# A fused attention, norm and gated feed-forward kernel: the second group's scores moved behind the first group, kept low bits on ScalarE, normalising on GpSimd

## The chip, the cores and the metric

The kernel runs on one core of a Trainium2 chip. The time is the device time of one execution in microseconds (us). Three runs of the kernel before took 690.78, 692.34 and 692.8 us; the median is 692.34. Engines: TensorE (PE) multiplies, VectorE (DVE) and ScalarE (ACT) work on whole tiles, GpSimd (POOL) does some of the same work, SyncE (SP) issues transfers. Each takes its own instructions in the order of the program and waits on semaphores for the others.

## The reference

Causal attention for batch 4, 12 heads, 448 positions, head size 64, float32, then a root-mean-square norm and a gated feed-forward layer over 1792 tokens of width 768 (inner width 1536). The weights arrive as float64.

```python
scores = scale * np.matmul(q, k.transpose(0, 1, 3, 2))
scores = np.where(mask, -1000000000.0, scores)
attn = np.exp(scores - np.max(scores, axis=-1, keepdims=True))
attn = attn / (np.sum(attn, axis=-1, keepdims=True) + 1e-09)
x = np.matmul(attn, v)          # then (batch, position, head * 64 + d)
rms = np.sqrt(np.mean(x * x, axis=-1, keepdims=True) + 1e-06)
xn = x / rms * rms_g
g = xn @ w_gate
silu = g * (1.0 / (1.0 + np.exp(-g)))
out = (silu * (xn @ w_val)) @ w_out
```

## The kernel before

**Data.** Activations lie feature-major: a tile has 128 features on its partitions and 512 tokens side by side. A float32 product is made of rounded parts: each operand is split into a high and a low part, and three matmuls (L438 to L440: high by high, low of x, low of w) make one multiplication of 128 x 128 by 512.

**Weights.** There are 36 tiles of 128 x 768, numbered s; tile s is loaded as float64 (two 32-bit words to a value) and turned into float32 by `convert_ops` (L367): c0 scales the high word (ScalarE, L377), c1 multiplies the high word by 0, which leaves its sign (GpSimd, L378), c2 joins to it three low bits, shifted out of the low word (VectorE, L380), c3 shifts the scaled value and joins those bits to it (VectorE, L382), and the result is also stored to DRAM. `split_w` (L387) then makes the high part w_h (ScalarE, L392) and the low part w_l (VectorE at L394 for even tiles, GpSimd by `pool_op` at L102 for odd ones).

**Attention.** The work is cut into 60 units, each for two heads and one stretch of queries, in three groups that end at units 12, 24 and 60; a group's tokens go through the norm and the feed-forward layer together. The first two groups have 256 queries a unit. One unit passes through `steps_s` (scores L191, mask and negative maximum L200, exponential and its sum L203, reciprocal of the sum L212, normalising L206 on ScalarE for units 15 to 23 and L208 on GpSimd for the others), `steps_t` (transposes L248, copies out of their banks L252 or L254) and `steps_a` (products L274, copy to x L289). x is squared and summed (`square`, `rms`: matmuls with ones L336, square root L338, then four reciprocals of 128 x 128 on VectorE, L341), and split into high and low parts (L327, L328).

**Order.** The order is written out by hand. `round_steps(p)` gives the steps of one round: scores of unit p+3, products of p, the two transposes of p+1. A main loop performs one step at a time and puts weight loads, conversions, splits and multiplications between the steps; `post(d, f)` puts an instruction d ticks later. During the first group the multiplications of tiles 0 to 2 that are ready go between the steps. The rounds run on until four steps past the first group's end; then the feed-forward stage begins: three slots to a weight tile, each with two of six multiplications, and the remaining attention steps of the second group are spread over the first 108 slots (L54). Gate tiles (even) give `gr` (L452), tanh (L453) and L454; value tiles (odd) give the gated product (L462), its high part hh (L463) and low part hl (L465). The sections behind the second group (the third group, the output products, lines L567 to L735) are not touched.

Of the kernel before, what the change touches and what calls it, by code (L numbers as in the profile page):

```python
# [61 lines left out]
def attention_ffn(ctx: ExitStack, tc: tile.TileContext, qk0, qk1, qk2, v, v2, w, g, out, out2):  # L62
# [108 lines left out]
    def steps_s(p):  # L171
# [22 lines left out]
        def softmax(e, i, pss):  # L194
# [10 lines left out]
            if ENDS[0] + 3 <= p < ENDS[1]:  # L205
                pr["norms"].append(lambda: nc.scalar.mul(sp, sp, rs))  # L206
            else:
                pr["norms"].append(lambda: nc.gpsimd.tensor_scalar(  # L208
                    sp, sp, rs, 1.0, op0=ALU.mult, op1=ALU.mult))
# [157 lines left out]
    def convert_ops(s):  # L367
        if s >= NU:
# [5 lines left out]
        hf_ = raw_w.bitcast(F32)[:, :, 1]  # L374

# [11 lines left out]
    def split_w(s):  # L387
        if s < 2 * NU:
            t = wt[s]
            h = ws_p.tile([P, DM], F32R, tag="wh", name="w_h")  # L390
            l = ws_p.tile([P, DM], F32R, tag="wl", name="w_l")
            nc.scalar.copy(h, t)  # L392
            if s % 2 == 0 and s < NU or s > NU + 2 * NF and s % 2:
                post(T["wl0" if s == 0 else "wl2" if s == 2 else "wl"], lambda: nc.vector.tensor_tensor(l, t, f32(h), op=ALU.subtract))  # L394
            else:
                post(T["wl0" if s == 1 else "wl"], lambda: pool_op(l, t, ALU.subtract, f32(h)))
            wt[s] = tuple(a.rearrange("p (k m) -> p k m", m=P) for a in (h, l))
            u = s - NU
# [339 lines left out]
    def round_steps(p):  # L738

        noop = [lambda: None]  # L740
        (s_, ts) = (f or noop for f in (steps_s(p + DP), steps_t(p + 1)))
# [16 lines left out]
        ts = (ts + noop)[:2]  # L758
        return [both] + ts if p > ENDS[0] else [scores, products, ts[0]] + 2 * noop + ts[1:]
# [31 lines left out]
    with tc.manual_schedule():  # L791
# [215 lines left out]
```

## Time and profile before

| what | before |
|---|---|
| median of three runs (lowest, highest) | 692.34 us (690.78, 692.8) |
| the profiled execution's own time | 691.18 us |
| its span, mean granted TensorE clock | 689.1 us, 0.993 |
| TensorE busy | 668.7 us (97%) |
| VectorE busy | 539.4 us (78%) |
| ScalarE busy | 371.4 us (54%) |
| GpSimd busy | 359.6 us (52%) |
| TensorE waits for GpSimd's low part of w (L440) | 5.0 us in 2 waits, longest 4.5 |
| TensorE waits for ScalarE's copy of transposes (L274) | 2.8 us in 2, longest 2.6 |
| TensorE waits for VectorE's copy of transposes (L274) | 2.7 us in 4, longest 1.4 |

The profile is of one execution; a row gives the start, the duration, the engine and the line of one or several instructions, and in brackets how long the engine stood idle before it and which engine's result ended that wait. The clock that the throttle granted TensorE is a share of full speed. Adding up busy time says little here, since the engines wait for each other; a wait of TensorE is what an edit can take away or bring.

### The profile page before, as it was taken

The numbers are of one execution on the slowest core, as the hardware profiler recorded it, in microseconds if no ns is written. First come the engines' busy times: TensorE is split into PE (matmuls) and PEld (weight loads), VectorE is DVE, ScalarE is ACT, GpSimd is POOL, SyncE is SP. The second block draws the span as 40 slices with busy tenths as digits, with TensorE's granted clock in tenths as the row PEclk, the third lists the DMA queues.
The fourth block names the chain that finished last, engine by engine and source line by source line (L and its number), as shares of the span: only waits on it lengthen the run. The fifth ranks groups of instructions, "written<-read, shape, count | busy, mean of one in ns | idle before, by whom it ended". The sixth has DMA issues, their size and how long they took to land. (4 is left out here: it accounts for less than half of the span.)

```text
span 689.1 us, 11935 instructions
## 1 busy us (share of the span) xinstructions
PE 668.7 (97%) x4108; PEld 550.9 (80%) x4108; DVE 539.4 (78%) x1030; ACT 371.4 (54%) x832; POOL 359.6 (52%) x311
## 2 busy tenths in 40 slices
PE   8879899999999999999999999999999999999997
PEld 6546577777777777687877777888999999999997
DVE  4967999999997667777686968389386868679993
ACT  6958877877694535355364544434434342455550
POOL 4979446555547544747576566663363536312220
PEclk9989999999999999999999999999999999999999
DMA  7655587878777746575758565324667566562641
GB/s 250 226 176 176 163 273 259 290 253 274 241 251 275 246 144 219 189 251 181 260 170 263 185 206 179 115 101 150 187 214 250 173 251 221 176 168 74 175 138 65
DMA packets 71355, 138.80 MB, mean 201 GB/s; under 512 B 7744, under 2 KB 39232, under 8 KB 71296
## 3 DMA queue, kind: packets, MB, share of 16 engines
q1 hardware_dynamic: 71296, 138.05, 60.8%
q8 instruction: 32, 0.52, 0.3%
q14 instruction: 27, 0.22, 0.1%
HBM read 104.21 MB, written 33.82 MB: 200 GB/s over the span
## 5 line engine op out<-in xcount | busy, mean ns | idle before, releaser
L208 POOL TENSOR_SCALAR sp<-sp,rs 128x384 f32<-128x384 f32 (+3 forms) x132 | 87.6, 681 | 101.2 <-DVE rs L212 93.2
L438 PE MATMUL m_ps<-xh,w_h 128*128 128x512 f32 x282 | 120.5, 427 | 1.7 <-DVE rs L212 1.7
L440 PE MATMUL m_ps<-xh,w_l 128*128 128x512 f32 x282 | 112.0, 397 | 4.5 <-POOL w_l L102 4.5
L203 ACT ACTIVATE sp<-sp,nm 128x384 f32<-128x384 f32 (+3 forms) x168 | 87.2, 524 | 47.2 <-DVE nm L200 47.2
L439 PE MATMUL m_ps<-xl,w_h 128*128 128x512 f32 x282 | 111.4, 395 | 0.0
L102 POOL TENSOR_TENSOR a_l<-w_q,a_h 128x768 fp32r<-128x768 f32 x24 | 47.6, 1985 | 66.5 <-ACT a_h L476 66.3
L378 POOL TENSOR_SCALAR w<-w 128x768 f32<-128x768 f32 x36 | 45.4, 1262 | 47.3 <-ACT w_c L377 47.3
L274 PEld LDWEIGHTS a_ps<-pt,v_r 128*64 128x64 f32 (+1 forms) x864 | 40.9, 138 | 33.5 <-issue 13.2
L440 PEld LDWEIGHTS m_ps<-xh,w_l 128*128 128x128 f32 x282 | 53.5, 190 | 17.0 <-POOL w_l L102 5.0
L438 PEld LDWEIGHTS m_ps<-xh,w_h 128*128 128x128 f32 x282 | 53.6, 190 | 14.2 <-issue 6.1
L274 PE MATMUL a_ps<-pt,v_r 128*64 128x128 f32 (+2 forms) x864 | 57.0, 269 | 7.4 <-ACT pt L254 2.8
L252 DVE COPY pt<-t_ps 128x384 f32<-128x384 f32 (+1 forms) x71 | 42.5, 598 | 26.6 <-PE t_ps L248 26.5
L102 POOL TENSOR_TENSOR w_l<-w_r,w_h 128x768 fp32r<-128x768 f32 x30 | 59.6, 1994 | 5.6 <-ACT w_h L392 5.3
L439 PEld LDWEIGHTS m_ps<-xl,w_h 128*128 128x128 f32 x282 | 53.8, 191 | 7.9
L200 DVE CUSTOM_DVE_ANT_0 sp<-s_ps,mask 128x128 f32<-128x128 f32 (+3 forms) x136 | 49.8, 416 | 13.1 <-PE s_ps L191 12.1
L438 PE MATMUL m_ps<-hh,w_h 128*128 128x512 f32 x144 | 58.2, 404 | 0.0
L440 PE MATMUL m_ps<-hh,w_l 128*128 128x512 f32 x144 | 56.5, 392 | 0.4 <-POOL w_l L102 0.4
L439 PE MATMUL m_ps<-hl,w_h 128*128 128x512 f32 x144 | 56.2, 390 | 0.0
L248 PE MATMUL t_ps<-ident,sp 128*128 128x128 f32 (+1 forms) x309 | 50.3, 276 | 0.1
L248 PEld LDWEIGHTS t_ps<-ident,sp 128*128 128x128 f32 (+1 forms) x309 | 38.0, 139 | 14.6 <-issue 2.3
L382 DVE SCALAR_TENSOR_TENSOR w_c<-w_c,w 128x768 int32<-128x768 int32 x36 | 48.3, 1342 | 0.8
L380 DVE SCALAR_TENSOR_TENSOR w<-w 128x768 int32<-128x768 int32 x36 | 44.9, 1246 | 4.9 <-POOL w L378 4.9
(178 smaller groups left out, 1694.1 us busy)
## 6 DMA issues: line engine op xcount, KB each, us to landing
w<-in_w SPq DMA_DIRECT2D x36, 768.0 KB, 5.3
w<-w_c SPq DMA_DIRECT2D x36, 384.0 KB, 2.7
w_r<-w SPq DMA_DIRECT2D x36, 384.0 KB, 4.8
qk_r<-in_qk SPq DMA_DIRECT2D x48, 256.0 KB, 4.2
qk_r<-in_qk SPq DMA_DIRECT2D x12, 512.0 KB, 5.8
v_r<-in_v SPq DMA_DIRECT2D x12, 448.0 KB, 5.4
v_r<-in_v SPq DMA_DIRECT2D x24, 192.0 KB, 3.3
wy<-w_r SPq DMA_DIRECT2D x24, 192.0 KB, 4.7
```

Of the source, the lines that this page charges most:

```text
L102: nc.gpsimd.tensor_tensor(out_, a, b, op=op)
L200: nc.vector.tensor_tensor_reduce(out=sp, in0=ps, in1=mk, scale=nsc, scalar=3.0e38, op0=ALU.add, op1=ALU.min, accum_out=nm)
L203: post(T["exp" if p >= ENDS[0] else "exp0"], lambda: nc.scalar.activation(sp, sp, AF.Exp, bias=nm, scale=-1.0, accum_out=sm))
L208: pr["norms"].append(lambda: nc.gpsimd.tensor_scalar(sp, sp, rs, 1.0, op0=ALU.mult, op1=ALU.mult))
L248: nc.tensor.transpose(ps[:kb, at: at + P], pr["sp"][e][:, o + kb * j: o + kb * (j + 1)], ident)
L274: nc.tensor.matmul(av_ps[e * D: (e + 1) * D, p % 2, q0: q0 + n], raw_v[p][:kb, h, j, e, :], pr["pt", e][:kb, a0: a0 + n], start=(j == 0), ...
L378: (T["c1"], lambda: nc.gpsimd.tensor_scalar(hf_, hf_, 0.0, 1.0, op0=ALU.mult, op1=ALU.mult)),
L380: (T["c2" if s >= 5 else "c20"], lambda: nc.vector.scalar_tensor_tensor(out=lo, in0=lo, scalar=29, in1=hi, op0=ALU.logical_shift_right, op ...
L382: (T["c3" if s >= 5 else "c30"], lambda: nc.vector.scalar_tensor_tensor(out=ti, in0=ti, scalar=3, in1=lo, op0=ALU.logical_shift_left, op1= ...
L438: nc.tensor.matmul(ps, wh[:, k, :], mh, start=(first and k == ks[0]), stop=False)
L439: nc.tensor.matmul(ps, wh[:, k, :], ml, start=False, stop=False)
L440: nc.tensor.matmul(ps, wl[:, k, :], mh, start=False, stop=(last and k == 5))
```

## The change

Four edits. (1) The scores of units 12, 13 and 14 leave the rounds 9 to 11, and unit 12's transposes leave round 11; they are issued by a new `refill` behind unit 11's products. Rounds from unit 12 on have three steps. The attention steps that are spread over the 108 slots are 42 instead of 36. (2) For the odd tiles from 5 to 35 (16 of 36) c2 is made on ScalarE: an activation reads the top byte of the low word and writes a 16-bit integer into the high word. For the others c2 stays on VectorE and writes the high word instead of the low one. (3) Units 15 to 23 are normalised on GpSimd like the others (36 instructions). (4) w_l of tile 1 is made on VectorE instead of GpSimd.

```diff
--- before.py
+++ after.py
@@ -11,6 +11,8 @@
 F32 = mybir.dt.float32
 F32R = mybir.dt.float32r
 I32 = mybir.dt.int32
+I16 = mybir.dt.int16
+U8 = mybir.dt.uint8
 BF16 = mybir.dt.bfloat16
 ALU = mybir.AluOpType
 AF = mybir.ActivationFunctionType
@@ -202,11 +204,8 @@
                 op0=ALU.add, op1=ALU.min, accum_out=nm)
             post(T["exp" if p >= ENDS[0] else "exp0"], lambda: nc.scalar.activation(
                 sp, sp, AF.Exp, bias=nm, scale=-1.0, accum_out=sm))
-            if ENDS[0] + 3 <= p < ENDS[1]:
-                pr["norms"].append(lambda: nc.scalar.mul(sp, sp, rs))
-            else:
-                pr["norms"].append(lambda: nc.gpsimd.tensor_scalar(
-                    sp, sp, rs, 1.0, op0=ALU.mult, op1=ALU.mult))
+            pr["norms"].append(lambda: nc.gpsimd.tensor_scalar(
+                sp, sp, rs, 1.0, op0=ALU.mult, op1=ALU.mult))
 
         def norm():
             nc.vector.reciprocal(pr["rs"][:, :nb], pr["sm"][:, :nb])
@@ -372,15 +371,22 @@
         wt[s] = t
         ti, lo, hi = t.bitcast(I32), raw_w[:, :, 0], raw_w[:, :, 1]
         hf_ = raw_w.bitcast(F32)[:, :, 1]
+        flat = raw_w.rearrange("p c t -> p (c t)")
+        low = flat.bitcast(I16).rearrange("p (c t) -> p c t", t=4)[:, :, 2]
+        top = flat.bitcast(U8).rearrange("p (c t) -> p c t", t=8)[:, :, 3]
+        if s >= 5 and s % 2:
+            kept = (T["c2"], lambda: nc.scalar.activation(low, top, AF.Copy, bias=-31.0 / 64, scale=1.0 / 32))
+        else:
+            kept = (T["c2" if s >= 5 else "c20"], lambda: nc.vector.scalar_tensor_tensor(
+                out=hi, in0=lo, scalar=29, in1=hi, op0=ALU.logical_shift_right, op1=ALU.bitwise_or))
 
         return [
             (T["c0"], lambda: nc.scalar.mul(t, hf_, 2.0 ** -112)),
             (T["c1"], lambda: nc.gpsimd.tensor_scalar(
                 hf_, hf_, 0.0, 1.0, op0=ALU.mult, op1=ALU.mult)),
-            (T["c2" if s >= 5 else "c20"], lambda: nc.vector.scalar_tensor_tensor(
-                out=lo, in0=lo, scalar=29, in1=hi, op0=ALU.logical_shift_right, op1=ALU.bitwise_or)),
+            kept,
             (T["c3" if s >= 5 else "c30"], lambda: nc.vector.scalar_tensor_tensor(
-                out=ti, in0=ti, scalar=3, in1=lo, op0=ALU.logical_shift_left, op1=ALU.bitwise_or)),
+                out=ti, in0=ti, scalar=3, in1=hi, op0=ALU.logical_shift_left, op1=ALU.bitwise_or)),
             (T["c5" if s >= 5 else "c50"], lambda: nc.sync.dma_start(out=w32[s], in_=t)),
         ]
 
@@ -390,10 +396,10 @@
             h = ws_p.tile([P, DM], F32R, tag="wh", name="w_h")
             l = ws_p.tile([P, DM], F32R, tag="wl", name="w_l")
             nc.scalar.copy(h, t)
-            if s % 2 == 0 and s < NU or s > NU + 2 * NF and s % 2:
-                post(T["wl0" if s == 0 else "wl2" if s == 2 else "wl"], lambda: nc.vector.tensor_tensor(l, t, f32(h), op=ALU.subtract))
+            if s == 1 or s % 2 == 0 and s < NU or s > NU + 2 * NF and s % 2:
+                post(T["wl2" if s == 2 else "wl0" if s < 2 else "wl"], lambda: nc.vector.tensor_tensor(l, t, f32(h), op=ALU.subtract))
             else:
-                post(T["wl0" if s == 1 else "wl"], lambda: pool_op(l, t, ALU.subtract, f32(h)))
+                post(T["wl"], lambda: pool_op(l, t, ALU.subtract, f32(h)))
             wt[s] = tuple(a.rearrange("p (k m) -> p k m", m=P) for a in (h, l))
             u = s - NU
             if 0 <= u < 2 * NF:
@@ -738,7 +744,8 @@
     def round_steps(p):
 
         noop = [lambda: None]
-        (s_, ts) = (f or noop for f in (steps_s(p + DP), steps_t(p + 1)))
+        first = p < ENDS[0]
+        s_, ts = (f(n) if not first or n < ENDS[0] else [] for f, n in ((steps_s, p + DP), (steps_t, p + 1)))
         as_ = steps_a(p)
 
         def products():
@@ -749,14 +756,22 @@
         def scores():
             if p + 2 > 0:
                 post(T["lv"], lambda: load_v(p + 2))
-            s_[0]()
+            for f in s_:
+                f()
 
         def both():
             scores()
             products()
 
-        ts = (ts + noop)[:2]
-        return [both] + ts if p > ENDS[0] else [scores, products, ts[0]] + 2 * noop + ts[1:]
+        ts = (ts + 2 * noop)[:2]
+        return [scores, products, ts[0]] + 2 * noop + ts[1:] if first else [both] + ts
+
+    def refill():
+
+        steps = []
+        for p in range(ENDS[0], ENDS[0] + DP):
+            steps += steps_s(p) + ([lambda: None] * 2 if p < ENDS[0] + DP - 1 else steps_t(ENDS[0]))
+        return steps
 
     def round_of_two(p):
 
@@ -802,6 +817,8 @@
             steps += round_steps(p)
             if p + 1 in ENDS:
                 ends.append(len(steps))
+            if p + 1 == ENDS[0]:
+                steps += refill()
         steps.append(lambda: steps_t(ENDS[1] + 1)[0]())
         for p in range(ENDS[1], len(UNITS), 2):
             steps += round_of_two(p)
```

In the changed kernel the same instructions have other line numbers: scores L193, mask L202, exponential L205, normalising L207, transposes L247, copies L251 and L253, products L273, norm reciprocals L340, c2 on ScalarE L378 and on VectorE L380, c0 L384, c1 L385, c3 L388, w_h L398, w_l L400 and L104, multiplications L444 to L446, gr L458, tanh L459, hh L469.

GpSimd in the rounds of the first group, before (sp_535 and sp_536 are unit 7's two score tiles, sp_596 is unit 8's; w_l_577 is tile 1's low part, xr_556 a tile of x):

```order
L208 TENSOR_SCALAR sp_535<-sp_535,rs_534 128x128
L208 TENSOR_SCALAR sp_535<-sp_535,rs_534 128x256
L208 TENSOR_SCALAR sp_536<-sp_536,rs_534 128x128
L208 TENSOR_SCALAR sp_536<-sp_536,rs_534 128x256
L102 TENSOR_TENSOR sq_633<-xr_556 128x512
L102 TENSOR_TENSOR acc_407<-acc_407,sq_633 128x512
L102 TENSOR_TENSOR w_l_577<-w_c_455,w_h_576 128x768
L208 TENSOR_SCALAR sp_596<-sp_596,rs_595 128x128
```

and after:

```order
L207 TENSOR_SCALAR sp_535<-sp_535,rs_534 128x128
L207 TENSOR_SCALAR sp_535<-sp_535,rs_534 128x256
L207 TENSOR_SCALAR sp_536<-sp_536,rs_534 128x128
L207 TENSOR_SCALAR sp_536<-sp_536,rs_534 128x256
L104 TENSOR_TENSOR sq_633<-xr_556 128x512
L104 TENSOR_TENSOR acc_407<-acc_407,sq_633 128x512
L207 TENSOR_SCALAR sp_596<-sp_596,rs_595 128x128
L207 TENSOR_SCALAR sp_596<-sp_596,rs_595 128x256
```

w_l_577 is gone from GpSimd's queue, and the next unit's normalising follows the sum at once.

VectorE around the four reciprocals of the first group's norm, before (w64_727 is the raw tile 5, gr_1075 the first gate product):

```order
L212 RECIPROCAL rs_950<-sm_949 128x4
L341 RECIPROCAL rms_1014<-rms_1014 128x128 x4
L452 TENSOR_TENSOR gr_1075<-m_ps_579,rms_1014 128x512
L212 RECIPROCAL rs_1018<-sm_1017 128x4
L454 SCALAR_TENSOR_TENSOR t_sb_1076<-t_sb_1076,gr_1075 128x512
L380 SCALAR_TENSOR_TENSOR w64_727<-w64_727 128x768
L382 SCALAR_TENSOR_TENSOR w_c_1063<-w_c_1063,w64_727 128x768
```

and after (sp_931 and sp_932 are unit 12's score tiles, sp_961 and sp_962 unit 13's):

```order
L202 ISA sp_932,nm_928<-s_ps_934,mask_104 128x256
L202 ISA nm_928 128x1
L340 RECIPROCAL rms_926<-rms_926 128x128 x4
L202 ISA sp_961,nm_958<-s_ps_963,mask_104 128x128
L202 ISA nm_958 128x1
L202 ISA sp_961,nm_958<-s_ps_963,mask_104 128x256
L202 ISA nm_958 128x1
L202 ISA sp_962,nm_958<-s_ps_964,mask_104 128x128
L202 ISA nm_958 128x1
L202 ISA sp_962,nm_958<-s_ps_964,mask_104 128x256
L202 ISA nm_958 128x1
L458 TENSOR_TENSOR gr_990<-m_ps_579,rms_926 128x512
```

Before, the masks of four units of the second group stand ahead of the reciprocals; after, those of unit 12 alone, and unit 13's stand behind them.

GpSimd at the same place, before (the names sp_951 and sp_952 belong to unit 14, w_l_1066 is tile 3's low part):

```order
L208 TENSOR_SCALAR sp_951<-sp_951,rs_950 128x128
L208 TENSOR_SCALAR sp_951<-sp_951,rs_950 128x256
L208 TENSOR_SCALAR sp_952<-sp_952,rs_950 128x128
L208 TENSOR_SCALAR sp_952<-sp_952,rs_950 128x256
L378 TENSOR_SCALAR w64_727<-w64_727 128x768
L102 TENSOR_TENSOR w_l_1066<-w_c_748,w_h_1065 128x768
L378 TENSOR_SCALAR w64_867<-w64_867 128x768
```

and after (sp_931 and sp_932 belong to unit 12, sp_961 to unit 13, w_l_981 is tile 3's low part):

```order
L385 TENSOR_SCALAR w64_608<-w64_608 128x768
L385 TENSOR_SCALAR w64_727<-w64_727 128x768
L104 TENSOR_TENSOR w_l_981<-w_c_748,w_h_980 128x768
L207 TENSOR_SCALAR sp_931<-sp_931,rs_930 128x128
L207 TENSOR_SCALAR sp_931<-sp_931,rs_930 128x256
L207 TENSOR_SCALAR sp_932<-sp_932,rs_930 128x128
L207 TENSOR_SCALAR sp_932<-sp_932,rs_930 128x256
L385 TENSOR_SCALAR w64_845<-w64_845 128x768
L207 TENSOR_SCALAR sp_961<-sp_961,rs_960 128x128
```

Unit 12's normalising now stands behind tile 3's low part.

ScalarE behind the square root, before (sp_1019 and sp_1020 are unit 15's tiles, pt_1085 a copy for unit 13's products):

```order
L377 ACTIVATE w_c_1063<-w64_727 128x768
L392 CAST w_h_1065<-w_c_748 128x768
L453 ACTIVATE t_sb_1076<-gr_1075 128x512
L206 ACTIVATE sp_1019<-sp_1019,rs_1018 128x128
L206 ACTIVATE sp_1019<-sp_1019,rs_1018 128x256
L206 ACTIVATE sp_1020<-sp_1020,rs_1018 128x128
L206 ACTIVATE sp_1020<-sp_1020,rs_1018 128x256
L254 COPY pt_1085<-x_ps_1086 128x384
L377 ACTIVATE w_c_1091<-w64_867 128x768
```

and after (sp_1020 and sp_1021 are unit 14's, w64_727 the raw tile 5, w_h_980 tile 3's high part):

```order
L384 ACTIVATE w_c_978<-w64_727 128x768
L398 CAST w_h_980<-w_c_748 128x768
L459 ACTIVATE t_sb_991<-gr_990 128x512
L384 ACTIVATE w_c_1000<-w64_845 128x768
L398 CAST w_h_1002<-w_c_857 128x768
L378 ACTIVATE w64_727<-w64_727 128x768
L469 CAST hh_1014<-t_sb_991 128x512
L205 ACTIVATE sp_1020,sm_1018<-sp_1020,nm_1017 128x128
L205 ACTIVATE sp_1020,sm_1018<-sp_1020,nm_1017 128x256
```

L378 is the kept low bits of tile 5, now on ScalarE, between tile 4's high part and the cast hh; L206, the normalising, is gone.

## Rows read from the trace of the kernel before

**Rows 1.** Busy times by stage: stretch, length, each engine busy (instructions), TensorE clock, DMA.

```profile
41.00:48.00 7.00, 6.15 (x27) 3.97 (x27) 2.84 (x12) 0.00 (x0) 2.65 (x6) 0.51 0.59 189
78.50:82.00 3.50, 3.50 (x9) 2.73 (x10) 3.47 (x7) 0.91 (x2) 0.86 (x1) 0.51 0.28 110
...
92.00:180.00 88.00, 88.00 (x452) 68.59 (x451) 87.67 (x132) 66.39 (x152) 49.29 (x30) 1.00 0.78 266
```

**Rows 2.** Timeline near 40 us: start, duration, engine, line, operation, [idle before, releaser].

```profile
38.23 1.91 DVE L382 SCALAR_TENSOR_TENSOR w_c<-w_c,w 128x768 int32<-128x768 int32 x1
...
39.28 2.52 POOL L102 TENSOR_TENSOR w_l<-w_c,w_h 128x768 fp32r<-128x768 f32 x1
...
41.85 0.80 PE L440 MATMUL m_ps<-xh,w_l 128*128 128x512 f32 x1 [4.54 <-POOL w_l L102]
...
44.60 0.56 DVE L252 COPY pt<-x_ps 128x384 f32<-128x384 f32 x1 [4.47 <-PE x_ps L248]
...
46.08 1.55 PE L274 MATMUL a_ps<-pt,v_r 128*64 128x256 f32 x8
```

**Rows 3.** Timeline from 66 to 78 us, all engines, behind the sum of squares.

```profile
66.89 1.02 PE L336 MATMUL t_ps<-acc,ones 128*128 128x512 f32 x2
...
69.77 0.29 DVE L200 CUSTOM_DVE_ANT_0 sp<-s_ps,mask 128x128 f32<-128x128 f32 x1 [1.51 <-PE s_ps L191]
...
70.81 0.40 ACT L203 ACTIVATE sp<-sp,nm 128x128 f32<-128x128 f32 x1
...
70.97 3.35 DVE L341 RECIPROCAL rms<-rms 128x128 f32<-128x128 f32 x4
...
71.25 1.62 POOL L208 TENSOR_SCALAR sp<-sp,rs 128x128 f32<-128x128 f32 x4 [3.53 <-DVE rs L212]
...
72.70 0.30 ACT L226 ACTIVATE sm<-sm,tiny 128x4 f32<-128x4 f32 x1
...
73.46 0.93 PE L191 MATMUL s_ps<-qk_r 64*128 64x128 f32 x8
...
75.38 1.80 POOL L102 TENSOR_TENSOR w_l<-w_c,w_h 128x768 fp32r<-128x768 f32 x1
75.69 1.48 ACT L206 ACTIVATE sp<-sp,rs 128x128 f32<-128x128 f32 x4
...
77.58 0.86 PE L274 MATMUL a_ps<-pt,v_r 128*64 128x256 f32 x6 [2.62 <-ACT pt L254]
```

**Rows 4.** Timeline of TensorE alone, 86 to 92 us.

```profile
86.57 0.49 PE L248 MATMUL x_ps<-ident,sp 128*128 128x128 f32 x3
...
91.20 0.47 PE L438 MATMUL m_ps<-xh,w_h 128*128 128x512 f32 x1 [1.38 <-DVE rs L212]
```

**Rows 5.** Groups by line, 0 to 240 us: count, busy us, mean ns, idle before.

```profile
L382 DVE SCALAR_TENSOR_TENSOR w_c<-w_c,w 128x768 int32<-128x768 int32 x36 | 48.3, 1342 | 0.8
...
L380 DVE SCALAR_TENSOR_TENSOR w<-w 128x768 int32<-128x768 int32 x36 | 44.9, 1246 | 4.9 <-POOL w L378 4.9
...
L377 ACT ACTIVATE w_c<-w 128x768 f32<-128x768 f32 x36 | 33.1, 919 | 10.2 <-DMA w<-in_w 8.0 <-issue 2.2
L392 ACT CAST w_h<-w_c 128x768 fp32r<-128x768 f32 x36 | 29.6, 823 | 0.7 <-DVE w_c L382 0.7
...
L453 ACT ACTIVATE t_sb<-gr 128x512 f32<-128x512 f32 x12 | 7.6, 631 | 6.1 <-DVE gr L452 5.8
L452 DVE TENSOR_TENSOR gr<-m_ps,rms 128x512 f32<-128x512 f32 x11 | 7.5, 680 | 0.1
```

**Rows 6.** Timeline near 116 us: VectorE and GpSimd.

```profile
115.75 2.13 POOL L102 TENSOR_TENSOR w_l<-w_c,w_h 128x768 fp32r<-128x768 f32 x1 [0.74 <-ACT w_h L392]
...
116.09 2.62 DVE L380 SCALAR_TENSOR_TENSOR w<-w 128x768 int32<-128x768 int32 x1
...
120.86 0.92 DVE L380 SCALAR_TENSOR_TENSOR w<-w 128x768 int32<-128x768 int32 x1
```

**Rows 7.** Groups by line, 92 to 180 us: TensorE, last of the three multiplications.

```profile
L440 PE MATMUL m_ps<-xh,w_l 128*128 128x512 f32 x107 | 41.9, 391 | 0.0
```

## The prediction

> **What bounds the kernel now.** I read the busy times by stage first, then the timelines of the three places that the change touches, then the groups by line. From 92 to 180 us TensorE is busy all of the 88.00 us, and VectorE 87.67 of them; ScalarE has 66.39, GpSimd 49.29 [rows 1]. So no edit gains in that stretch: a lighter VectorE gives TensorE nothing that it waits for there, and an edit can only cost. What can be gained lies before 92 us. There TensorE waits 4.54 us for the low part of weight tile 1, which GpSimd makes last of a row of jobs [rows 2], then 2.62 us ahead of unit 13's products and 1.38 us ahead of a bank of the gate products [rows 3, 4]. Behind the first two waits the granted clock is 0.51 (the lower of the two levels, 1.2 GHz): from 41 to 48 us and from 78.5 to 82 us [rows 1].
>
> All sums are on the profiled execution (691.18 us: a span of 689.1 and 2.1 around it). The median of the timed runs, 692.34, is 1.2 above it, the lowest run 0.4 below.
>
> **Before the first group's end.** The low part of tile 1 leaves GpSimd (2.52 us [rows 2]) for VectorE, where a step on a tile takes 0.92 with nothing in the way [rows 6], 0.95 with the gap to the next; it is then done near 34.6 us, and the wait of 4.54 goes, with the low clock behind it. Late next is VectorE: the conversions of tile 2 ended at 38.23 + 1.91 = 40.14 [rows 2], now 0.95 later, and behind them stands the copy of 0.56 for unit 7's products, so 41.65, against 46.08 before: 4.3 us gained. From there to the matmuls that sum the squares before took 66.89 - 46.08 = 20.8 us. Three scores leave that stretch (each 0.93 by its row [rows 3], 0.86 without its overlap with the next) and two sets of transposes (each 0.49 by its row [rows 4], 0.25 without the overlap): 3.1 us of TensorE, of which other waits keep 0.8. So 18.5, and the sum of squares at 60.25 instead of 66.89: 6.6 us earlier. The 3.1 are only moved.
>
> **The refill.** Let T be 60.25. Before, unit 15's scores stood here and unit 12's transposes were long done. Now the pipeline of unit 12 starts from nothing, in a fixed order on each engine. TensorE: sums 1.8, scores of 12 to T+2.7. VectorE: masks of 12 (1.2: 69.77 to 70.97 [rows 3]; the last scores are awaited) to +4.1, then, as the order shows, the four reciprocals of the norm, 3.35 together [rows 3], to +7.4, and only then the masks of 13, to +8.65. Scores of 14 need the bank that those masks read: TensorE stands some 1.9 us. ScalarE: the exponentials of 13 (2.2 for a unit: 70.81 to 73.0 [rows 3]) start with their first mask and end at +9.95, conversion 0.92, high part 0.82 [rows 5], +11.7. GpSimd: the low part of tile 3 (1.80 [rows 3]) stands ahead of the normalising of unit 12: +13.5, and half of the 1.62 [rows 3] makes +14.4. There the first transposes of unit 12 wait in TensorE's queue, some 5.0 us, and the multiplications behind them that are ready wait with them. The second wait follows: unit 12's products need a copy on ScalarE that stands behind tanh 0.63, conversion 0.92, high part 0.82, kept bits 0.92 (+15.0); VectorE 0.92, 0.92 and the gated product 0.68 (+17.5); then ScalarE's cast 0.63, exponentials 2.2, 0.92, 0.82, a copy of about 0.5, 0.63, 0.92, 0.92 and 0.5: +25.5 [rows 3, 5, 6]. TensorE has until then scores, transposes and 27 multiplications, some 0.23 apart (an estimate: three of them in 0.82 with attention's share, 88.00/107 [rows 7]), in all 7.5 us: to +21.9, and then stands 3.6. With 0.8 for the products: T+26.3 = 86.6 us. At that moment the same parts of tile 4 are done, by the order, as before at 86.57 [rows 4], but attention owes a score group (0.86), one unit's products (0.8) and three sets of transposes (0.75): 2.4 us. So the gain of 6.6 has become a loss of 86.6 + 2.4 - 86.57 = 2.5 us. Before's own 1.38 [rows 4] then goes, and TensorE, which has stood 5 us, is likely to run on at the lower clock as it did after 2.62 us of waiting: 3.50 us at 0.51 instead of 1.00 [rows 1] cost 1.7. Nearly 2.8 behind, after 1.9 + 5.0 + 3.6 us of waits against 4.0 before. Bounds: -3.5 (all of the refill hidden, 3.1 of 6.6 given back) to +5.
>
> **The steady stretch.** 16 of 36 steps that make the kept low bits go from VectorE to ScalarE, and 36 normalising multiplications (9 units) from ScalarE to GpSimd. ScalarE loses 9 x 1.48 = 13.3 us [rows 3] and gets 16 of a form that no row shows (bytes in, 16-bit words out, 768 to a partition). Nearest are the scaling with the same stride of 8 bytes, 0.92, and the cast, 0.82 [rows 5]; the upper bound is VectorE's 1.34 for the step behind it [rows 5]. I take 0.92: 14.7 us; at 1.34, 6.7 more. For ScalarE an exchange of equals, and VectorE is relieved of 16 x 0.92 to 1.25, 15 to 20 us.
>
> The price is the order. Now tile n's kept bits stand on ScalarE, and VectorE, which goes in order, waits there for them; ScalarE waits a few rows on for VectorE's results. For two tiles the loop is, on VectorE the gate product 0.68; on ScalarE tanh 0.63, high part 0.82, conversion 0.92, kept bits 0.92; on VectorE finish 0.92, product 0.68, kept bits 0.92, low part 0.92, finish 0.92 [rows 5, 6]: 8.3, with 0.78 of a unit's masks [rows 3] and small steps (some 1.4 us a unit) 9.4. TensorE's two tiles take 88.00 x 12/107 = 9.9 [rows 7]. While VectorE's steps run at 0.92 there is no slip; at the means of 1.25 and 1.34 [rows 5], 0.4 more on two or three of them, it is 10.2 to 10.6. Ten such loops: 0 to 7 us; I take 2, by the nearer end, and -0.6 for three small waits that the lighter VectorE ends. **Sum:** 2.8 + 2 - 0.6, some +4 us: 695.2 on the profiled execution, 695.5 with a part of the 1.2.
>
> What drives those means up is in the trace: the same kept-bits step took 2.62 us beside GpSimd's subtraction of 2.13, and 0.92 alone [rows 6]. The Trainium skill ("SBUF — State Buffer", "🔬 SBUF: two separate sides") says that VectorE with two SBUF inputs and GpSimd share a port pair "for the whole instruction; the other fully blocks". The trace agrees, with its 2.62 against 0.92. By that rule 9 x 1.62 = 14.6 us of normalising can block what the 15 us of kept bits relieve, which is the third rival.
>
> **Rivals.** (1) *The two cancel.* The refill's queue is shorter than I count, by the 3.6 of its last wait: if the copy does not come out behind ScalarE's chain, the sum is +4 - 3.6: about 692. For it: TensorE has multiplications in plenty there; against: they stand behind the transposes. (2) *Faster.* The refill hides in the work that TensorE has: 6.6 gained, 3.1 given back, 0.6 of small waits: 691.2 - 4.1 = 687. For it speaks that both waits that go are real [rows 2, 3]; against it that VectorE's 3.35 us of reciprocals and GpSimd's low part now stand in front of the only unit in the pipeline. It decides if unit 12's transposes come before T+10. (3) *The lock.* Normalising on GpSimd, 36 times, falls beside VectorE's steps, so that they stay at 1.34 and more though there are fewer; every loop takes 10.9 instead of 9.9 and ten loops cost 9.5 instead of 2: 702.5. For it: the 2.62 of [rows 6]; against: VectorE has 15 us of room. (4) That ScalarE's new form costs the 1.34 and more: 16 x 0.42 = 6.7 of ScalarE, of which ten loops carry 4.2: 699.7, inside the forecast's chance.
>
> **How the numbers follow.** Forecast 0.42 (its own range 692.5 to 699), cancel 0.22, faster 0.27, lock 0.09. Within 0.3%, what a measurement can tell from no change, is 690.3 to 694.4. Of the forecast 0.30 lie above it, 0.10 inside, 0.02 below; of cancel 0.18 inside and 0.04 below. Slower 0.30 + 0.09 = 0.39; same 0.28; faster 0.27 + 0.06 = 0.33. The range, 686.5 to 701, leaves out the lock's far end (0.08) and the far side of faster (0.1).
>
> **What would show it.** Right: no wait for tile 1's low part, unit 7's products at 41 to 42 us, the sum of squares near 60, then waits of 2, 5 and 3 to 4 us for unit 13's masks, 12's normalising and 12's copy, with clock 0.5 behind them, and from 92 to 180 us small waits for the kept bits' tile. Wrong early: the sum of squares after 63 us. Wrong in the refill: no wait above 2 us between 60 and 87. Wrong in the steady stretch: TensorE still at 88.00 of 88 (slip 0, 693), or waits of more than 5 us there (the lock).

## The result and the profile after

| | before | after |
|---|---|---|
| median of 14 runs each (lowest, highest) | 692.62 us (690.12, 695.42) | 696.56 us (693.88, 699.34) |
| ratio after to before, 95% interval | | 1.0058 [1.0039, 1.0078] |
| the profiled execution, its span | 691.18, 689.1 us | 698.23, 696.4 us |

The change makes the kernel 4 us slower; 695.5 was forecast. The two profiled executions lie 7.0 apart, one 1.4 below its median and one 1.7 above. The last 2.2 of that arise behind 490 us, where the program is the same in both. Ratios are of fast executions: one of e10's six (929.28 us, mean granted clock 0.655) and one of the 18 of the kernel before that ran beside e9 to e11 (798.1 us, 0.777) are left out of them.

The busy times by stage, after (columns as in [rows 1]):

```profile
41.00:48.00 7.00, 6.65 (x43) 4.54 (x43) 5.45 (x25) 5.93 (x20) 6.25 (x10) 1.00 0.83 282
74.50:78.50 4.00, 4.00 (x11) 3.08 (x12) 3.03 (x3) 0.93 (x1) 2.70 (x4) 0.53 0.31 98
92.00:180.00 88.00, 87.10 (x444) 66.93 (x442) 64.33 (x122) 71.46 (x138) 51.90 (x52) 1.00 0.74 252
```

The low clock of 41 to 48 us is gone, and one at 74.5 to 78.5 us is there. In the steady stretch VectorE has fallen from 87.67 to 64.33 us, and TensorE, which did not stand there, does so for 0.9.

TensorE's waits, after: releaser, us in total, times, longest:

```profile
PE t_ps L247 <- POOL sp L207: 5.2, 2, 4.8
...
PE a_ps L273 <- ACT pt L253: 3.3, 3, 1.9
...
PE s_ps L193 <- DVE nm L202: 1.7, 2, 1.3
...
PE m_ps L444 <- DVE t_sb L468: 0.9, 3, 0.4
```

The wait for tile 1's low part [rows 2] is gone. In its place stand three in the refill: 1.3 us for VectorE's masks, 4.8 for GpSimd's normalising and 1.9 for ScalarE's copy. The timeline after, of unit 7's products and of the refill:

```profile
41.14 0.86 PE L273 MATMUL a_ps<-pt,v_r 128*64 128x256 f32 x6 [0.77 <-DVE pt L251]
...
60.38 1.02 PE L335 MATMUL t_ps<-acc,ones 128*128 128x512 f32 x2
...
64.26 3.38 DVE L340 RECIPROCAL rms<-rms 128x128 f32<-128x128 f32 x4
...
67.56 0.23 DVE L202 CUSTOM_DVE_ANT_0 sp<-s_ps,mask 128x128 f32<-128x128 f32 x1
...
68.19 1.47 PE L193 MATMUL s_ps<-qk_r 64*128 64x128 f32 x8 [1.28 <-DVE nm L202]
...
69.99 0.87 ACT L384 ACTIVATE w_c<-w 128x768 f32<-128x768 f32 x1
70.76 0.82 ACT L398 CAST w_h<-w_c 128x768 fp32r<-128x768 f32 x1
...
71.78 1.82 POOL L104 TENSOR_TENSOR w_l<-w_c,w_h 128x768 fp32r<-128x768 f32 x1
...
73.52 1.91 ACT L378 ACTIVATE w<-w 128x768 int16<-128x768 uint8 x1
73.59 2.06 POOL L207 TENSOR_SCALAR sp<-sp,rs 128x128 f32<-128x128 f32 x4
...
74.45 1.15 PE L247 MATMUL t_ps<-ident,sp 128*128 128x128 f32 x3 [4.78 <-POOL sp L207]
...
75.47 0.98 DVE L388 SCALAR_TENSOR_TENSOR w_c<-w_c,w 128x768 int32<-128x768 int32 x1 [1.31 <-ACT w L378]
...
84.47 1.94 ACT L378 ACTIVATE w<-w 128x768 int16<-128x768 uint8 x1
86.14 0.59 ACT L253 COPY pt<-x_ps 128x384 f32<-128x384 f32 x1
...
86.78 0.86 PE L273 MATMUL a_ps<-pt,v_r 128*64 128x256 f32 x6 [1.89 <-ACT pt L253]
```

This answers to [rows 3]. The sum of squares starts at 60.38, as forecast (60.25). Behind it the four reciprocals (64.26) hold unit 13's masks until 67.56; ScalarE's conversion and high part follow its exponentials; GpSimd's low part of tile 3 (71.78) ends at 73.6; the normalising of unit 12 begins there, and TensorE has stood 4.78 us. At 75.47 VectorE's last conversion step has waited 1.31 for ScalarE's kept bits, which took 1.91 us. At 86.14 the copy for unit 12's products comes out behind the next such step (84.47, 1.94 us), and TensorE has stood 1.89.

Groups by line, after, 0 to 240 us (columns as in [rows 5]):

```profile
L388 DVE SCALAR_TENSOR_TENSOR w_c<-w_c,w 128x768 int32<-128x768 int32 x36 | 40.4, 1123 | 40.4 <-ACT w L378 40.2
...
L378 ACT ACTIVATE w<-w 128x768 int16<-128x768 uint8 x16 | 31.2, 1950 | 0.0
```

ScalarE's kept bits take 1.95 us each, and VectorE waits 40.2 us for them in all.

**Where TensorE loses.** I count the matmuls of the feed-forward multiplications (three to a multiplication) as n, and take the start of the n-th less the work of all TensorE instructions that began before it, at intervals read from stretches at the full clock (0.2275 us a matmul, 0.86 a unit's scores, 0.80 its products, 0.25 a set of transposes). That is time lost, whatever the order. Worked out from each trace, less the same of the kernel before (us; the names are those of the experiments below):

```
                              n=40   n=100   n=360   n=640
after                         -3.4    +1.7    +4.1    +5.2
e1  low part of tile 1 only   -5.7    -5.7    -5.7    -5.4
e2  moved scores only         +0.9    +6.9    +7.1    +6.8
e9  both                      -3.4    +2.1    +2.4    +2.8
e3  after, bits on VectorE    -3.7    +1.7    +2.2    +4.2
e4  after, bits as float32    -4.1    -1.4    -1.1    -2.1
e6  after, refill reordered   -3.4    +1.6    +2.5    +2.4
e5  after, no moved scores    -5.0    -1.5    -1.7    -2.4
e10 e5 with bits as float32   -6.3    -7.1    -7.3    -8.6
e7  e1 and GpSimd normalising -5.0    -2.8    -0.9    +1.2
e11 e1, one normalising late  -5.1    -2.5    -2.7    -3.7
e12 e1, last step late        -4.8    -5.1    -3.3    -4.0
```

n=40 is the first group's end, n=100 lies behind the refill (93 us after), n=360 at 169 us, n=640 at 250 us. The changed kernel gains 3.4, loses 5.1 in the refill and 3.5 behind it, 2.4 of them up to n=360.

Each row is of one profiled execution. Most lie within 1 us of their medians, but after's lies 1.7 above, e12's 1.9 and e7's 2.1 above, e5's 2.3 and e10's 3.1 below: the table shows where time is lost, and the ratios below how much.

### The profile page after: what moved, and what is told of

It is laid out like the page before. It is cut to its first block, busy times and chain, and to the rows that moved or that the text cites. A ratio compares the mean times of both kernels' runs of the same rounds, so it can differ in the third digit from the quotient of the medians.

```text
span 696.4 us, 11917 instructions
## 1 busy us (share of the span) xinstructions
PE 671.7 (96%) x4108; PEld 551.0 (79%) x4108; DVE 509.5 (73%) x1015; ACT 387.2 (56%) x812; POOL 372.9 (54%) x346
## 5 line engine op out<-in xcount | busy, mean ns | idle before, releaser
L207 POOL TENSOR_SCALAR sp<-sp,rs 128x384 f32<-128x384 f32 (+3 forms) x168 | 113.7, 693 | 107.6 <-DVE rs L211 99.2
L444 PE MATMUL m_ps<-xh,w_h 128*128 128x512 f32 x282 | 120.1, 426 | 0.9 <-DVE t_sb L468 0.9
L205 ACT ACTIVATE sp<-sp,nm 128x384 f32<-128x384 f32 (+3 forms) x168 | 87.1, 521 | 43.5 <-DVE nm L202 43.4
L446 PE MATMUL m_ps<-xh,w_l 128*128 128x512 f32 x282 | 111.2, 394 | 0.0
L104 POOL TENSOR_TENSOR a_l<-w_q,a_h 128x768 fp32r<-128x768 f32 x24 | 47.2, 1966 | 66.8 <-ACT a_h L482 65.1
L273 PEld LDWEIGHTS a_ps<-pt,v_r 128*64 128x64 f32 (+1 forms) x864 | 42.0, 137 | 35.4 <-issue 11.1
L388 DVE SCALAR_TENSOR_TENSOR w_c<-w_c,w 128x768 int32<-128x768 int32 x36 | 40.4, 1123 | 40.4 <-ACT w L378 40.2
L273 PE MATMUL a_ps<-pt,v_r 128*64 128x128 f32 (+2 forms) x864 | 59.3, 268 | 8.7 <-DVE pt L251 4.1
L444 PEld LDWEIGHTS m_ps<-xh,w_h 128*128 128x128 f32 x282 | 53.3, 189 | 14.1 <-issue 3.8
L446 PEld LDWEIGHTS m_ps<-xh,w_l 128*128 128x128 f32 x282 | 53.1, 188 | 12.1
L104 POOL TENSOR_TENSOR w_l<-w_r,w_h 128x768 fp32r<-128x768 f32 x30 | 59.6, 1994 | 5.6 <-ACT w_h L398 5.4
L251 DVE COPY pt<-t_ps 128x384 f32<-128x384 f32 (+1 forms) x71 | 42.4, 597 | 26.1 <-PE t_ps L247 25.9
L444 PE MATMUL m_ps<-hh,w_h 128*128 128x512 f32 x144 | 58.4, 405 | 0.0
L202 DVE CUSTOM_DVE_ANT_0 sp<-s_ps,mask 128x128 f32<-128x128 f32 (+3 forms) x136 | 49.6, 412 | 11.3 <-PE s_ps L193 10.3
L385 POOL TENSOR_SCALAR w<-w 128x768 f32<-128x768 f32 x36 | 37.5, 1043 | 36.7 <-ACT w_c L384 34.7
L446 PE MATMUL m_ps<-hh,w_l 128*128 128x512 f32 x144 | 56.3, 391 | 0.0
L247 PE MATMUL t_ps<-ident,sp 128*128 128x128 f32 (+1 forms) x309 | 50.9, 277 | 5.4 <-POOL sp L207 5.2
L247 PEld LDWEIGHTS t_ps<-ident,sp 128*128 128x128 f32 (+1 forms) x309 | 38.1, 138 | 20.4 <-POOL sp L207 7.9
L193 PE MATMUL s_ps<-qk_r 64*128 64x128 f32 (+3 forms) x296 | 43.8, 426 | 1.9 <-DVE nm L202 1.7
```

The lines of the kernel that those rows point to most:

```text
L104: nc.gpsimd.tensor_tensor(out_, a, b, op=op)
L193: nc.tensor.matmul(ps, r[:, q0: q0 + nq], r[:, k0: k0 + wd], start=True, stop=True)
L202: nc.vector.tensor_tensor_reduce(out=sp, in0=ps, in1=mk, scale=nsc, scalar=3.0e38, op0=ALU.add, op1=ALU.min, accum_out=nm)
L205: post(T["exp" if p >= ENDS[0] else "exp0"], lambda: nc.scalar.activation(sp, sp, AF.Exp, bias=nm, scale=-1.0, accum_out=sm))
L207: pr["norms"].append(lambda: nc.gpsimd.tensor_scalar(sp, sp, rs, 1.0, op0=ALU.mult, op1=ALU.mult))
L247: nc.tensor.transpose(ps[:kb, at: at + P], pr["sp"][e][:, o + kb * j: o + kb * (j + 1)], ident)
```

## The experiments

All ratios are to the kernel before, run on the same chip; differences between two versions are those of their ratios, times 692.3 us.

**e1: the low part of tile 1 on VectorE, nothing else.**

```diff
-if s % 2 == 0 and s < NU or ...:
+if s == 1 or s % 2 == 0 and s < NU or ...:
```

> The kernel before with one edit alone: the low part of tile 1 on VectorE. Theory A (this edit is a gain of its own, and what follows it loses more): the wait of 4.54 us and the low clock behind it go, unit 7's products start near 41.7 us, nothing is moved to later, so 3 to 4.4 us faster than before, ratio 0.9935 to 0.9960. Rival (the first group is limited by other queues): the waits ahead of unit 13's products and behind them grow by what is gained, within 1 us of before.

687.39 us, ratio 0.9928 [0.9906, 0.9949]: 5 us faster, a little more than expected. The 2.62 us wait is as long as before and comes 5.7 us earlier.

**e2: the moved scores, nothing else; e9: both.** `round_steps` and `refill` as in the change, over the kernel before (e2) and over e1 (e9).

> The kernel before with the moved scores alone: units 12 to 14 begin behind unit 11's products, low part of tile 1 still on GpSimd, kept bits on VectorE, units 15 to 23 normalised on ScalarE. Theory A: the refill costs by itself; the 4.54 us stay, three scores are moved, then waits of about 1.3, 5 and 2 us against 2.6 and 1.4 before, so 3 to 6 us slower than before, ratio 1.0045 to 1.0085. Rival (the moved scores cost nothing, the kept bits and the normalising do): within 1 us of before.

> The kernel before with two edits: tile 1's low part on VectorE and the moved scores; kept bits on VectorE, units 15 to 23 normalised on ScalarE. Theory A (the edits add: -5.0 and +6.9): 693 to 695.5 us, ratio 1.001 to 1.0045; the normalising on GpSimd and the kept bits on ScalarE then make up what is left to the changed kernel, 1.5 to 3 us. Rival (with tile 1 in time, the refill hides): 690 us or less, ratio 0.9975 or below.

e2: 699.08 us, 1.0101 [1.0080, 1.0123], more than expected. e9: 694.53 us, 1.0040 [1.0025, 1.0055], as expected; what the other two edits add to it, 1.2 us, is less than the 1.5 to 3 expected. TensorE in e9, from the timeline:

```profile
68.20 1.48 PE L191 MATMUL s_ps<-qk_r 64*128 64x128 f32 x8 [1.29 <-DVE nm L200]
75.23 0.47 PE L248 MATMUL t_ps<-ident,sp 128*128 128x128 f32 x1 [5.55 <-POOL sp L208]
77.20 0.69 PE L248 MATMUL t_ps<-ident,sp 128*128 128x128 f32 x2 [1.50 <-POOL sp L208]
```

The refill's waits are there with the kept bits on VectorE and the normalising of units 15 on left on ScalarE. The moved scores cost 7.0 us alone and, by e9 less e1, 7.8 with tile 1 in time.

**e3: the changed kernel, all kept bits on VectorE.** `if s >= 5 and s % 2:` becomes `if False:`.

> The changed kernel with the kept low bits of all tiles on VectorE, the other three edits as they are. Theory A (ScalarE's form takes 1.95 us and VectorE waits for it, 40 us in all): TensorE loses about 1 us in place of 3.5 from 92 to 240 us, so 2.5 to 3.5 us faster than the changed kernel, ratio to before 1.0008 to 1.0022. Rival (the normalising on GpSimd holds VectorE up): the time stays with the changed kernel's, 1.005 to 1.0065, since VectorE has more steps again beside GpSimd's.

695.63 us, 1.0046 [1.0028, 1.0065]: 0.8 us faster than the changed kernel, which the intervals do not tell apart. Theory A's number is missed, and the rival's 1.005 lies inside the interval. The long step is real all the same, as e4 and e8 show: giving VectorE back its 16 steps costs nearly what ScalarE's long ones did.

**e4: the changed kernel, ScalarE's step as a float32 copy; e10: the same without the moved scores.**

```diff
-nc.scalar.activation(low, top, AF.Copy, bias=-31.0 / 64, scale=1.0 / 32)
+nc.scalar.activation(hf_, hf_, AF.Copy, bias=0.0, scale=1.0)
```

> The changed kernel, but ScalarE's step on the odd tiles copies the high word in place as float32 instead of reading a byte and writing a 16-bit word: those tiles lose their three low bits, the order of all instructions stays. Theory A with the duration as cause: the step takes 0.9 to 1.0 us in place of 1.95, and 2 to 3 us are gained on the changed kernel, ratio to before 1.0015 to 1.003. Rival (the order is the cause, VectorE waits for ScalarE whatever the step takes): within 1 us of the changed kernel, 1.0045 to 1.0065.

> The changed kernel without the moved scores, and ScalarE's step as a float32 copy in place (the odd tiles lose their three low bits). Theory A (the 16-bit write is what ScalarE's queue can't carry; the order alone gains): the wait of 5.4 us at 87.7 us goes or falls below 2, 686 to 688.5 us, ratio 0.991 to 0.9955. Rival (the normalising on GpSimd makes that wait, as it made one of 4.1 us with the kept bits on VectorE): 690 us or more, ratio 0.997 or above.

e4: 690.41 us, 0.9970 [0.9956, 0.9983]; e10: 685.91 us, 0.9912 [0.9890, 0.9935]. Groups by line in e4 (0 to 240 us), then the products of unit 12 in its timeline:

```profile
L388 DVE SCALAR_TENSOR_TENSOR w_c<-w_c,w 128x768 int32<-128x768 int32 x36 | 45.1, 1254 | 24.9 <-ACT w L378 24.7
...
L378 ACT ACTIVATE w<-w 128x768 f32<-128x768 f32 x16 | 14.4, 901 | 0.0
```

```profile
83.28 1.29 PE L273 MATMUL a_ps<-pt,v_r 128*64 128x256 f32 x8
```

With the order untouched and the step at 0.90, e4 is 6.1 us faster than the changed kernel, twice what was expected: by the table 0.7 before the refill, 2.4 in it and 4.2 behind. So the duration is the cause of these, not the order, though VectorE still waits 24.7 us for ScalarE. The 1.89 us wait of unit 12's products is gone. And against e3, which has the same steps on VectorE, e4 is 5.3 us faster. In e10 a wait of 3.5 us near 84 us is left, more than the 2 expected; the ratio lies in the expected range all the same.

**e8: four forms of that step by turns on the odd tiles** (one execution).

> The changed kernel with four forms of ScalarE's step by turns on the odd tiles: float32 to float32 in place; float32 to a 16-bit word; a byte to float32; a byte to a 16-bit word as in the changed kernel. The first three write zeros or the old value, so those tiles lose their low bits and some their signs. Theory A (the write of a 16-bit word is what doubles the duration): 0.9, 1.95, 0.9, 1.95 us. Rival B (the read of a byte): 0.9, 0.9, 1.95, 1.95. Rival C (either alone is cheap and only the pair is slow): 0.9, 0.9, 0.9, 1.95.

The groups by line, costliest first (byte to 16 bits, float32 to 16 bits, float32 to float32, byte to float32):

```profile
L386 ACT ACTIVATE w<-w 128x768 int16<-128x768 uint8 x4 | 7.8, 1954 | 0.0
L382 ACT ACTIVATE w<-w 128x768 int16<-128x768 f32 x4 | 7.8, 1947 | 0.0
...
L380 ACT ACTIVATE w<-w 128x768 f32<-128x768 f32 x4 | 3.6, 902 | 0.0
L384 ACT ACTIVATE w<-w 128x768 f32<-128x768 uint8 x4 | 3.6, 888 | 0.0
```

Both forms that write a 16-bit word take 1.95 us, both that write float32 0.89 to 0.90, all with the same stride of 8 bytes: theory A.

**e5: the changed kernel without the moved scores.**

> The changed kernel with the scores of units 12 to 14 back in rounds 9 to 11; the other three edits stay. Theory A (the moved scores cost about 7 us, ScalarE's step of 1.95 us costs 3 to 5 in the steady stretch, tile 1's low part gains 5.5): 688 to 691 us, ratio 0.994 to 0.998, with no wait of TensorE above 3 us between 60 and 80 us. Rival (ScalarE's longer step and the normalising cost the most, and would do so without the refill): 693 us or more, ratio 1.001 or above.

692.15 us, 0.9993 [0.9976, 1.0010]: 4.5 us faster than the changed kernel, but between theory and rival. Without the refill a wait of 5.44 us near 87.7 us appears, for a bank (the memory that TensorE writes a product to) that VectorE's gated product reads and so frees:

```profile
71.24 0.86 PE L273 MATMUL a_ps<-pt,v_r 128*64 128x256 f32 x6 [1.23 <-ACT pt L253]
...
87.71 0.77 PE L444 MATMUL m_ps<-xh,w_h 128*128 128x512 f32 x1 [5.44 <-DVE rs L211]
```

The bracket names a short reciprocal that VectorE ended last; the gated product ends just ahead of it (86.88 + 0.68), and TensorE starts 0.15 us behind that end, as it does, within 0.01, at the like waits of e1, e7, e10 and e11. Ahead of the product VectorE itself had stood 2.20 us for ScalarE's kept bits, in e10 1.17.

**e6: the changed kernel, the refill in another order.** Unit 12's reciprocal and normalising come four ticks behind its scores instead of seven, the norm's reciprocals three or four ticks later.

```diff
-post(i if b else 1, lambda sl=sl: nc.vector.reciprocal(...))
+post(i if b else 4 + i // 2, lambda sl=sl: nc.vector.reciprocal(...))
-post(T["norm1" if kind else "norm0"], norm)
+post(T["norm1" if kind else "norm0"] if p != ENDS[0] else 4, norm)
```

> The changed kernel with another order in the refill alone: unit 13's masks ahead of the norm's four reciprocals, unit 12's normalising ahead of tile 3's low part on GpSimd. Theory A (the two waits come from what stands ahead in VectorE's and GpSimd's queues): the wait of 1.3 us for the masks goes, the one of 4.8 for the normalising goes and leaves one of 2 to 3 for tile 3's low part, 2 to 3.5 us faster than the changed kernel, ratio 1.001 to 1.003. Rival (the pipeline of one unit is simply too long, whatever the order): within 1 us of the changed kernel.

694.54 us, 1.0034 [1.0015, 1.0053], 1.7 us faster than the changed kernel, a little less than expected, with intervals that meet. TensorE's waits in the refill:

```profile
68.68 0.89 PE L247 MATMUL t_ps<-ident,sp 128*128 128x128 f32 x3 [0.89 <-POOL sp L207]
...
72.76 0.50 PE L446 MATMUL m_ps<-xh,w_l 128*128 128x512 f32 x1 [1.30 <-POOL w_l L104]
...
81.74 1.11 PE L273 MATMUL a_ps<-pt,v_r 128*64 128x256 f32 x2 [2.07 <-ACT pt L253]
85.21 1.54 PE L273 MATMUL a_ps<-pt,v_r 128*64 128x256 f32 x6 [2.35 <-ACT pt L253]
```

The 1.28 is gone and the 4.78 has become 0.89 and 1.30: what stood ahead in VectorE's and GpSimd's queues made them. But the time goes into two waits of 2.07 and 2.35 for copies on ScalarE, behind its long steps: by n=100 nothing is gained, and the table puts what is gained behind that.

**e7: e1, and units 15 to 23 normalised on GpSimd.**

> The kernel before with two edits: tile 1's low part on VectorE, and units 15 to 23 normalised on GpSimd. Theory A (the normalising stood ahead of unit 13's copy on ScalarE, 1.48 us, and nothing waits for GpSimd): the wait of 2.62 us becomes some 1.1, 0.5 to 1.5 us faster than the first edit alone, ratio 0.991 to 0.9925. Rival (GpSimd's normalising holds up VectorE's steps in the steady stretch): 1 us or more slower than the first edit alone, ratio 0.9945 or above.

692.07 us, 0.9995 [0.9979, 1.0010]: 4.6 us slower than e1, the rival. TensorE's waits, from the timelines of 70 to 92 and 140 to 190 us:

```profile
71.18 0.86 PE L271 MATMUL a_ps<-pt,v_r 128*64 128x256 f32 x6 [1.24 <-ACT pt L251]
...
85.96 0.76 PE L435 MATMUL m_ps<-xh,w_h 128*128 128x512 f32 x1 [4.12 <-DVE rs L209]
```

```profile
149.81 0.47 PE L435 MATMUL m_ps<-xh,w_h 128*128 128x512 f32 x1 [1.76 <-DVE rs L209]
...
181.01 0.47 PE L435 MATMUL m_ps<-xh,w_h 128*128 128x512 f32 x1 [1.18 <-DVE rs L209]
```

The first wait shrinks from 2.62 to 1.24 as theory A had it. The later ones are for banks that VectorE's gated product frees. This execution is the slowest of the twelve. Groups by line from 92 to 180 us, VectorE's kept bits in e1 (first) and in e7:

```profile
L380 DVE SCALAR_TENSOR_TENSOR w<-w 128x768 int32<-128x768 int32 x18 | 24.2, 1347 | 0.0
```

```profile
L377 DVE SCALAR_TENSOR_TENSOR w<-w 128x768 int32<-128x768 int32 x17 | 25.3, 1486 | 3.9 <-POOL w L375 3.9
...
L205 POOL TENSOR_SCALAR sp<-sp,rs 128x256 f32<-128x256 f32 x10 | 9.1, 908 | 0.0
```

The step takes 1.49 instead of 1.35 us and waits 3.9 us for GpSimd's sign step, which in e1 it does not there; a normalising of 128 x 256 takes 0.91 there, against 0.60 in the first 240 us of the kernel before.

**e11: e1, unit 15's normalising one tick later, still on ScalarE.** `post(T[...] + (p == ENDS[0] + DP), norm)`.

> A version meant to beat both: the kernel before with tile 1's low part on VectorE and unit 15's normalising, which stays on ScalarE, one tick later, behind the copy that unit 13's products wait for. Theory A (the four multiplications of 1.48 us stand in that wait): the wait of 2.62 us becomes some 1.1, 0.5 to 2 us faster than the first edit alone, ratio 0.990 to 0.992. Rival (the delay is handed on: tanh's gate product and the banks behind it come later): within 0.5 us of the first edit alone, 0.992 to 0.994, with the 1.39 us wait for a bank grown.

688.78 us, 0.9958 [0.9943, 0.9972]: not faster than e1 but 2.1 us slower, outside both ranges, though the intervals just overlap. The rival's sign, the longer wait for a bank, is there. TensorE in e1, then in e11:

```profile
71.92 1.03 PE L274 MATMUL a_ps<-pt,v_r 128*64 128x256 f32 x6 [2.62 <-ACT pt L254]
...
85.52 0.47 PE L438 MATMUL m_ps<-xh,w_h 128*128 128x512 f32 x1 [1.39 <-DVE rs L212]
```

```profile
71.16 0.86 PE L274 MATMUL a_ps<-pt,v_r 128*64 128x256 f32 x6 [1.25 <-ACT pt L254]
...
86.28 0.76 PE L438 MATMUL m_ps<-xh,w_h 128*128 128x512 f32 x1 [4.47 <-DVE rs L212]
```

The first wait is 1.25 instead of 2.62, and the clock does not fall behind it; TensorE arrives 2.3 us earlier (n=60 by its trace) and then stands 4.47 instead of 1.39 for the bank. The bank is freed by VectorE's gated product, which there ends at 86.1 us: VectorE's queue sets the pace at 86 us, whatever TensorE gains before. That end comes 0.8 us later than in e1 (85.37), and behind the longer wait the clock is low (0.52 from 86.28 to 91.9 us, in e1 1.00 from 85.5): by n=100 e11 stands at -2.5, e1 at -5.7.

**e12: e1, VectorE's last conversion step one tick later.** `c3=5, c5=7` become `c3=6, c5=8`.

> A version meant to beat the first edit alone: tile 1's low part on VectorE, and VectorE's last conversion step of the tiles from 5 on one tick later, so that the gated product stands ahead of it in VectorE's queue. Theory A (TensorE's 1.39 us wait near 85 us is for a bank that the gated product frees, and 1.50 us of the last conversion step stand ahead of it): that wait goes, 0.5 to 1.5 us faster than the first edit alone, ratio 0.990 to 0.9922. Rival (the converted tiles come later and the waits move to the high and low parts of the weights): 1 us or more slower than the first edit alone, ratio 0.9945 or above, with waits for the parts of w in the steady stretch.

686.11 us, 0.9914 [0.9893, 0.9935]: the fastest version that keeps the whole computation, 6 us faster than before, though not told apart from e1 (0.9928). Its trace does not show the reason that I gave: the 1.39 us wait is gone, but the gated product ends no earlier (84.74 + 0.67 against 84.70 + 0.67 us); in this execution TensorE only comes later, and a wait of 1.72 stands at 117.8 us. Part of that lateness is the clock: behind the same wait of 2.62 us it is low for 6.3 us here (0.50 from 72.8 to 79.1) and for 3.7 in e1 (0.58 from 71.9 to 75.6).

## Why the prediction was right, and where it was not

**Early part.** As forecast: unit 7's products start at 41.14 us (41.65 forecast), the sum of squares at 60.38 (60.25). e1 shows that this edit alone is the gain. Two slips in these sums change nothing: 46.08 less 41.65 is 4.4, not 4.3, and 41.65 + 18.5 is 60.15.

**Refill.** The place and the releasers were right. e2 and e9 show that the moved scores bring the first two waits by themselves, and e6 shows their causes: masks behind the reciprocals, normalising behind tile 3's low part. The third is a copy behind ScalarE's chain. The waits are 1.28, 4.78 and 1.89 against 1.9, 5.0 and 3.6; the low clock is there (0.53 for 4 us, 1.9 us by the working that gave 1.7). From n=40 to n=100 the refill loses 5.1 where the sum had 6.3 (from -3.5 to +2.8).

**Steady stretch.** Forecast +1.4, measured +3.5 in one execution. The term that was mis-sized is the unknown operation: 0.92 was taken, the upper bound was 1.34, and it is 1.95. Neither neighbour wrote 16-bit words. The loop that was to carry it was priced too high: with 1.95 in place of 0.92 its 9.4 us become 10.4, against TensorE's 9.9, some 5 us in ten loops, where the table has 2.4 from n=100 to n=360.

**Luck in the number.** e4 is the case that the sum was made for: the order of the changed kernel, and a step of 0.90 where the sum took 0.92. It takes 690.41 us, 5 below the 695.5, and is a little faster than the kernel before; the table has -4.1, -1.4 and -2.1 where the sum had -3.5, +2.8 and +4.2. So with its own size of the step the sum was too high in the refill by 3.6 us, where the third wait of 3.6 is not there at all, and behind it by 2.1. The true step of 1.95 put 6.1 us back. These errors have opposite signs, and that the measured 696.56 lies 1.1 from the forecast is luck. That the change is slower at all hangs on that step.

**A step that holds, but not as far as it was used.** "A lighter VectorE gives TensorE nothing" was said of 92 to 180 us, and against the kernel before it holds there. Busy times by stage of e4 and of e7 (columns as in [rows 1]):

```profile
92.00:180.00 88.00, 88.00 (x461) 68.21 (x461) 72.14 (x132) 67.85 (x149) 59.39 (x57) 1.00 0.78 265
```

```profile
92.00:180.00 88.00, 86.07 (x434) 67.14 (x432) 79.82 (x119) 56.03 (x124) 61.52 (x49) 1.00 0.72 249
```

With VectorE at 72 us of 88 in e4 (the same in e10), TensorE has the same 88.00 as before, and e4 and e10 gain at most 0.2 us from n=100 to n=360. But the sum credits VectorE's relief with 0.6 us in all, and that is too little: e4 against e3 and e10 against e7 differ in where the kept bits are made, at 0.90 us, and by 5.3 and 5.7 us. For e4 against e3 the table puts 2.7 of that in the refill, 0.2 from n=100 to n=360 and 3.0 behind; for e10 against e7 3.0, 2.1 and 3.4, there with two executions that lie 11 us apart. So the relief pays where TensorE has waits, before 92 us, in e7's steady stretch and behind 170 us. Some 2 us of e10's lead (an estimate: half of 4.1 us) is the clock, which stayed full behind its wait of 3.49 us and was at 0.50 from 85.9 to 90 us behind e7's 4.12. What gains behind 170 us was not followed up.

**Rivals.** *The lock* was priced as if it came on top. Normalising on GpSimd costs 4.6 us in e7 over e1, but 0.4 in e3 over e9, inside the intervals, though both keep all kept bits on VectorE; so a full VectorE alone does not make the price. Nor is all of e7's 4.6 GpSimd's doing: e11, which normalises on ScalarE, has the same long wait at 86 us with the low clock behind it, and stands at -2.5 at n=100, where e7 stands at -2.8 and e1 at -5.7. Over e11, e7 loses 2.6 us, part of it a wait for GpSimd's queue rather than for a port. How much is the one and how much the other was not tried. *The refill hides* is refuted by e9. *The two cancel* needed the refill's third wait to go: with the step at 1.95 us it is 1.89, with the step at 0.90 (e4) it is gone and the time is 690.4, near that rival's 692. *The new form costs 1.34 and more* came true, at 1.95; its price, 699.7 at 1.34 already, did not.

The four edits, each put on the ones before it, come to -5.0 for tile 1's low part (e1), +7.8 for the moved scores (e9 less e1), +0.4 for the normalising (e3 less e9) and +0.8 for the kept bits on ScalarE (the changed kernel less e3); the last two lie inside the intervals. With the step at 0.90 the last is -5.3 (e4 less e3).

## What to carry to other kernels

An operation that the trace does not show has to be bounded by the type that it writes too, or be timed by itself before it goes into a loop of engines. When TensorE shows 88 of 88 us, relieving the engine beside it gives nothing there, but it may give where TensorE waits, and loading that engine further may cost: price it stage by stage. A total near the forecast proves little: run the case that the sum was made for. Scores moved behind a group's end start an empty pipeline, and what stands ahead of its first unit in every queue is then on the path.

## What the runs showed of the hardware

ScalarE writing 16-bit integers at a stride of 8 bytes takes 1.95 us for 128 x 768, over twice the 0.90 of float32 at the same stride, whether it reads bytes or float32. Whether the type or the narrow write at that stride doubles it was not tried. The clock behind a wait, from the busy times by stage (columns as in [rows 1]) of e11, behind 1.25 and behind 4.47 us of waiting (1.00 is the level of 2.4 GHz, 0.50 that of 1.2 GHz):

```profile
71.20:74.20 3.00, 3.00 (x16) 2.25 (x17) 3.00 (x3) 2.82 (x6) 2.25 (x2) 1.00 0.01 3
86.30:89.30 3.00, 3.00 (x8) 1.96 (x10) 3.00 (x4) 3.00 (x7) 1.23 (x1) 0.50 0.99 324
```

and of e10, behind 3.49 us:

```profile
84.00:87.00 3.00, 2.95 (x20) 1.96 (x22) 3.00 (x4) 1.74 (x3) 2.84 (x3) 1.00 0.98 305
```

and of e1, behind 2.62 us:

```profile
72.00:75.00 3.00, 3.00 (x11) 2.14 (x12) 2.97 (x4) 1.43 (x2) 0.91 (x1) 0.58 0.00 0
```

TensorE ran on at the low level behind 4.47 us in e11, mostly at it behind 2.62 in e1, and at the full one behind 1.25 in e11 and 3.49 in e10; what tells the last from the others is open.
